# A second head's scores moved by 384 columns in a three-bank PSUM tile, and computed with one matmul fewer

## The chip, the cores and the metric

One core of one Trainium2 chip runs the whole program. The metric is the device time of one execution in microseconds (us). PE is the matrix engine (TensorE), PEld its weight loads, DVE the vector engine, ACT the scalar engine, POOL the GpSimd engine, and SP the engine that issues most DMAs. Matmul results land in PSUM, which here is used in banks of 512 fp32 columns; DVE and ACT read it from there.

## What is computed

Attention on 4 batches, 8 heads, 576 positions and head dimension 64, and behind it two dense stages on the 2304 rows that come out:

```python
q_rot, k_rot = rotate(q), rotate(k)
scores = (1 / sqrt(D)) * q_rot @ k_rot.T            # 576 x 576 for each head
attn = exp(scores - max); attn = attn / (sum + 1e-9)
x = attn @ v                                         # then (B*S) x (H*D) = 2304 x 512
h = maximum(maximum(x @ w1, x @ w2), x @ w3)         # 2304 x 768
x = h @ w_out                                        # 2304 x 512
h = x @ w_in; g = h * sigmoid(h)                     # 2304 x 2048
out = g @ w_out2                                     # 2304 x 512
```

## The kernel before

**Attention.** Heads go in pairs (`hp`, four for a batch): head 0 of a pair lies on partitions 0 to 63 of a tile `T`, head 1 on partitions 64 to 127. The 576 queries of a pair are cut into five tiles, `t` = 0 to 4; the first four have 128 queries for both heads, the fifth (`t` = 4) holds the last 64 queries of both heads and is treated as one head. That makes 16 pairs x 5 = 80 score tiles, 64 of them with two heads. The 576 keys are 512 "main" keys (columns 512 to 1023 of `T`) and 64 left over, which lie for both heads, block-diagonal, in a small tile `K`.

`tile_scores` (L349) computes a two-headed tile into the PSUM tile `s`, 128 partitions x 1536 columns, three banks, of which there is one buffer (`ps_s`, L93). Before, head 0 takes columns 0 to 575 and head 1 columns 576 to 1151. One matmul (L361) with `K` on all 128 partitions gives the 64 leftover columns of both heads, which are neighbours (512 to 639). L364 gives the main keys with 64 partitions for each head: 512 columns for head 0, and for head 1 384 columns (640 to 1023, the end of bank 1) and 128 columns (1024 to 1151, in bank 2). All of it is fp32, and the trace records every fp32 matmul of this kind twice, as two passes, each with a weight load of its own; so L361 has 64 x 2 and L364 has 64 x 3 x 2 records. `t` = 4 tiles use L354 and L355 instead.

`tile_max` (L370) takes the maximum of both heads with one DVE instruction (L374), then one ACT instruction per head computes the exponentials out of PSUM (L381) into the SBUF tile `e` (columns by `HK`, 576 a head). `tile_norm` scales `e` (L393), `tile_turn` transposes it on PE (L408, L413, L422) and evacuates (`pt`, L426, L428), `av` multiplies by V (L437, L441). `qk_turn` (L319) transposes q and k (L328, L334) for the next pair.

**Dense stages.** `moe1` (L510) is fed between the attention steps, by a counter of matmul columns (L947); it is the work that PE does while a score tile waits for its maximum and its exponentials. Its results leave PSUM by L526 and L528 on ACT and DVE. The second dense stage (L778 to L809) begins after the attention and after the last of `moe1`, at about 650 us of the trace.

**What sets the order.** The program is written in one sequence; a scheduler then gives each engine its own row of instructions, by a model of how long each takes. So a change in one matmul can move instructions of other steps past each other on every engine. Within one engine the row is fixed.

Of the kernel before, what the change touches and what calls it, by code (L numbers as in the profile page):

```python
# [11 lines left out]
AF = mybir.ActivationFunctionType  # L12
ALU = mybir.AluOpType
AX = mybir.AxisListType
# [8 lines left out]
def fused_kernel(  # L23
# [22 lines left out]
    nc = tc.nc  # L46
# [297 lines left out]

    s_t, e_t, sum_t, pt_t, exps = {}, {}, {}, {}, []
    HK = (slice(0, 576), slice(576, 1152))
    evacs = [0]

    def tile_scores(key):  # L349
        b, hp, t = key  # L350
        T, K, Q = T_t[b, hp]
        s = ps_s.tile([P, 1536], F32, tag="s", name="s")
        if t == 4:
            nc.tensor.matmul(s[:, 0:512], Q, T[:, 512:1024], start=True, stop=True)  # L354
            nc.tensor.matmul(s[:, 512:576], Q, T[:, 1024:1088], start=True, stop=True)  # L355
            s_t[key] = s
            return
        n = P
        qs = T[:, t * P:t * P + n]
        kt = T[:, 512:1024]  # L360
        nc.tensor.matmul(s[0:n, 512:640], qs, K, start=True, stop=True)  # L361
        for g, o, a, m in ((0, 0, 0, 512), (1, 640, 0, 384), (1, 1024, 384, 128)):
            r = slice(64 * g, 64 * g + 64)
            nc.tensor.matmul(s[0:n, o:o + m], qs[r], kt[r, a:a + m], start=True, stop=True)  # L364
        s_t[key] = s

    def heads(key):
        return 1 if key[2] == 4 else 2

    def tile_max(key):  # L370
        s = s_t.pop(key)
        m = heads(key)
        nb = small.tile([P, 2], F32, tag="nb", name="nb")
        x = nc.vector.tensor_reduce(  # L374
            out=nb[:, 0:m], in_=s[:, 0:576 * m].rearrange("p (h k) -> p h k", h=m), op=ALU.max, axis=AX.X, negate=True
        )
        last["max"] = x.ins
        e = e_p.tile([P, 1152], F32, tag="e", name="e")
        sm = small.tile([P, 2], F32, tag="sm", name="sm")
        for g in range(m):  # L380
            x = nc.scalar.activation(  # L381
                out=e[:, HK[g]], in_=s[:, HK[g]], func=AF.Exp, bias=nb[:, g:g + 1], accum_out=sm[:, g:g + 1]
            )
        exps.append(x.ins)
        e_t[key], sum_t[key] = e, sm

    def tile_norm(key):
# [4 lines left out]
        for g in range(m):  # L392
            nc.scalar.activation(out=e[:, HK[g]], in_=e[:, HK[g]], func=AF.Copy, scale=r[:, g:g + 1])  # L393

# [85 lines left out]
    def attention():  # L480

        for j in range(len(tiles) + 4):
            if j < len(tiles):
                tile_scores(tiles[j])
                tile_max(tiles[j])
            if 1 <= j <= len(tiles):
                tile_norm(tiles[j - 1])
            if 2 <= j <= len(tiles) + 1:
                tile_turn(tiles[j - 2])
            for f, a in events.pop(j, ()):  # L490
                f(*a)
            yield
# [206 lines left out]
    o = 0  # L699
    while o < NT:  # L700
        n = min(512, NT - o)
# [262 lines left out]
    n = 0  # L964
# [63 lines left out]
```

## Time and profile before

| | us |
|---|---|
| median of 3 runs | 1078.11 |
| lowest and highest of them | 1073.08, 1078.49 |
| the profiled execution, its own time | 1072.23 |
| its span (first to last instruction) | 1070.5 |
| PE busy in the span | 984.0 (92%) |
| DVE, ACT, POOL busy | 595.0, 592.0, 370.2 |
| mean granted TensorE clock | 0.971 |

Busy times of PE are unions of overlapping records: matmuls are pipelined, and one record begins before the one ahead of it has ended. What a matmul costs PE is therefore read from the start of one group of instructions to the start of the next, not from the mean duration of a record. The granted clock is 1 at 2.4 GHz and 0.5 at 1.2 GHz.

### The profile page before, as it was taken

What the parts mean: (1) busy time and instruction counts of PE and PEld (TensorE: products, weight loads), DVE (VectorE), ACT (ScalarE), POOL (GpSimd) and SP (SyncE); (2) the same over time, 40 slices, a digit from 0 to 9 for tenths busy, and PEclk for the clock granted to TensorE, in tenths of its full rate; (3) what the DMA queues carried; (4) which work ended last, traced back from release to release, by engine and by line L of the source; (5) the groups of instructions that cost most, each with busy time, mean ns of one, the idle gap of its engine ahead of it and who ended that gap; (6) DMA issues with size and microseconds to landing.
All of it is one profiled execution on the core that took longest, in us unless ns stands there. A gap on an engine that the chain in (4) does not pass through costs nothing.

```text
span 1070.5 us, 19191 instructions
## 1 busy us (share of the span) xinstructions
PE 984.0 (92%) x7554; PEld 761.6 (71%) x7554; DVE 595.0 (56%) x1078; ACT 592.0 (55%) x1298; POOL 370.2 (35%) x396
## 2 busy tenths in 40 slices
PE   2378897999998999989999999999999999999997
PEld 1245574676776677667767567778888888888887
DVE  5858667544476666476456559654532533533432
ACT  3668775646665767756666756464433433433432
POOL 1596125730115741032111211144343433433432
PEclk9678998999999999999999999998999999999999
DMA  7633022310225433223323326110100200100000
GB/s 193 204 111 111 30 90 57 82 24 1 73 85 146 122 95 90 72 73 86 122 60 89 115 68 248 49 64 1 60 10 12 60 16 6 40 21 1 21 21 20
DMA packets 81129, 76.28 MB, mean 71 GB/s; under 512 B 44944, under 2 KB 61840, under 8 KB 80528
## 3 DMA queue, kind: packets, MB, share of 16 engines
q1 hardware_dynamic: 77328, 64.77, 20.7%
q10 hardware_dynamic: 3712, 10.29, 2.9%
q8 instruction: 59, 0.97, 0.4%
q14 instruction: 30, 0.25, 0.1%
HBM read 57.21 MB, written 17.83 MB: 70 GB/s over the span
## 4 chain that ended last, share of the span: by engine, by line
PE 71%; DVE 5%; DMA 3%; POOL 1%; issue 1%; SPq 1%; ACT 1%; DVEq 0%; POOLq 0%; ACTq 0%
PE m L510 18%; PE mb L778 8%; PE m L778 8%; PE xp L441 5%; PE a L809 4%; PE c L809 4%; PE s L364 4%; PE b L809 4%; PE tr L422 4%; PE mg L510 3%; PE d L809 2%; PE xp L437 1%; PE s L361 1%; PE tr L328 1%; PE s L354 1%
## 5 line engine op out<-in xcount | busy, mean ns | idle before, releaser
L785 POOL TENSOR_TENSOR gs<-gs 128x256 f32<-128x256 f32 x144 | 131.4, 913 | 222.0 <-ACT gs L779 216.5
L510 PE MATMUL m<-x,w 128*128 128x256 f16 (+1 forms) x1380 | 197.8, 289 | 6.0 <-DVE t L528 3.2
L510 PEld LDWEIGHTS <-w 128*128 128x128 f16 x1632 | 158.6, 99 | 53.1 <-issue 13.0
L791 DVE SCALAR_TENSOR_TENSOR g<-gs,sg,g 128x768 f16<-128x768 f32 x72 | 97.9, 1362 | 173.4 <-ACT g L790 173.0
L778 PEld LDWEIGHTS <-wi 128*128 128x128 f16 x1656 | 162.0, 98 | 18.7
L809 PEld LDWEIGHTS <-g 128*128 128x128 f16 x1485 | 146.1, 99 | 21.5 <-DVE g L791 3.3
L207 POOL TENSOR_SCALAR z<-z 128x256 uint16<-128x256 uint16 x64 | 54.2, 847 | 256.6 <-DVE z L206 242.1
L374 DVE TENSOR_REDUCE nb<-s 128x2 f32<-128x1152 f32 (+1 forms) x80 | 98.7, 1234 | 63.1 <-PE s L364 48.4
L381 ACT ACTIVATE e<-s,nb 128x576 f32<-128x576 f32 x144 | 105.3, 737 | 46.3 <-DVE nb L374 42.0
L790 ACT ACTIVATE g<-gs,sg 128x768 f16<-128x768 f32 x72 | 74.9, 1041 | 72.2 <-POOL gs L785 71.1
L393 ACT ACTIVATE e<-e,rec 128x576 f32<-128x576 f32 x144 | 104.3, 768 | 17.9 <-DVE rec L391 17.7
L422 PE MATMUL tr<-ident,e 128*128 128x128 f32 x576 | 98.0, 287 | 12.1 <-ACT pt L426 3.1
L778 PE MATMUL mb<-yt,wi 128*128 128x256 f16 x828 | 95.0, 273 | 0.0
L778 PE MATMUL m<-yt,wi 128*128 128x256 f16 x828 | 94.8, 273 | 0.0
L422 PEld LDWEIGHTS tr<-ident,e 128*128 128x128 f32 x576 | 68.6, 145 | 32.8 <-ACT pt L426 5.8
L426 ACT ACTIVATE pt<-tr 128x384 f32<-128x384 f32 x128 | 61.1, 488 | 50.2 <-PE tr L422 49.8
L441 PE MATMUL xp<-pt,vd 128*64 128x256 f32 (+1 forms) x512 | 85.3, 427 | 0.0
L364 PE MATMUL s<-T 64*128 64x512 f32 (+2 forms) x384 | 82.1, 510 | 0.0
L510 PE MATMUL m<-h,wo 128*128 128x256 f16 (+1 forms) x448 | 64.9, 286 | 2.3 <-POOL wo L156 1.2
L364 PEld LDWEIGHTS s<-T 64*128 64x128 f32 x384 | 45.9, 196 | 27.3 <-issue 5.6
L779 ACT ACTIVATE gs<-mb,ch 128x512 f32<-128x512 f32 x36 | 24.7, 686 | 71.9 <-PE mb L778 71.9
L441 PEld LDWEIGHTS xp<-pt,vd 128*64 128x64 f32 x512 | 37.1, 140 | 35.0 <-issue 17.7
(199 smaller groups left out, 1500.0 us busy)
## 6 DMA issues: line engine op xcount, KB each, us to landing
z<-in_moe_w_in_dram SPq DMA_DIRECT2D x32, 256.0 KB, 3.2
z<-in_moe_w_out_dram SPq DMA_DIRECT2D x32, 256.0 KB, 3.2
w<-in_moe_w_dram ACTq DMA_DIRECT2D x6, 768.0 KB, 7.5
wo<-in_moe_w_dram ACTq DMA_DIRECT2D x6, 768.0 KB, 5.5
qk<-in_q_dram SPq DMA_DIRECT2D x32, 128.0 KB, 3.1
qk<-in_k_dram SPq DMA_DIRECT2D x32, 128.0 KB, 3.0
vd<-in_v_dram SPq DMA_DIRECT2D x16, 256.0 KB, 3.0
zwi<-z SPq DMA_DIRECT2D x32, 128.0 KB, 3.1
```

Source lines behind the costliest of these rows:

```text
L364: nc.tensor.matmul(s[0:n, o:o + m], qs[r], kt[r, a:a + m], start=True, stop=True)
L374: x = nc.vector.tensor_reduce(out=nb[:, 0:m], in_=s[:, 0:576 * m].rearrange("p (h k) -> p h k", h=m), op=ALU.max, axis=AX.X, negate=True)
L381: x = nc.scalar.activation(out=e[:, HK[g]], in_=s[:, HK[g]], func=AF.Exp, bias=nb[:, g:g + 1], accum_out=sm[:, g:g + 1])
L393: nc.scalar.activation(out=e[:, HK[g]], in_=e[:, HK[g]], func=AF.Copy, scale=r[:, g:g + 1])
L422: nc.tensor.transpose(tr[:, i * n:(i + 1) * n], e[0:n, c * P:(c + 1) * P], ident[0:n, 0:n])
L441: nc.tensor.matmul(xp[r, 0:n], v4[:, g, c, :], pt[:, c + 5 * g, :], start=False, stop=(c == 3))
L510: nc.tensor.matmul(ps[:, 0:n], l, r, start=(i == 0), stop=(i == len(passes) - 1))
L778: nc.tensor.matmul(ps[:, e * 256:e * 256 + 256], l, r, start=(i == 0), stop=(i == len(passes) - 1))
L785: nc.gpsimd.tensor_tensor(out=g[o], in0=g[x], in1=g[y], op=op)
L790: nc.scalar.activation(out=h, in_=x, func=AF.Copy, scale=sg)
L791: nc.vector.scalar_tensor_tensor(out=l, in0=x, scalar=sg, in1=h, op0=ALU.mult, op1=ALU.subtract)
L809: x = nc.tensor.matmul(ps, l, r, start=first, stop=last_, skip_group_check=True)
```

## The change

Head 1's scores stand in columns 960 to 1535: its 64 leftover columns at 960 to 1023, at the end of bank 1, and its 512 main columns at 1024 to 1535, which is bank 2. Its main keys take one matmul of 512 columns in place of 384 + 128. The matmul of the leftover keys now writes two runs of 64 columns, 448 apart (512 to 575 and 960 to 1023). The maximum reads two runs of 576 columns that begin 960 apart, and the exponentials of head 1 read from 960; `e` in SBUF keeps its layout. Tiles with `t` = 4 are as before.

```diff
+    SK = (slice(0, 576), slice(960, 1536))
+
+    def both(s, o, step, n):
+
+        return bass.AP(tensor=s.tensor, offset=s.offset + o, ap=[list(s.ap[0]), [step, 2], [1, n]])
...
-        nc.tensor.matmul(s[0:n, 512:640], qs, K, start=True, stop=True)
-        for g, o, a, m in ((0, 0, 0, 512), (1, 640, 0, 384), (1, 1024, 384, 128)):
+        nc.tensor.matmul(both(s, 512, 448, 64), qs, K, start=True, stop=True)
+        for g, o in ((0, 0), (1, 1024)):
             r = slice(64 * g, 64 * g + 64)
-            nc.tensor.matmul(s[0:n, o:o + m], qs[r], kt[r, a:a + m], start=True, stop=True)
+            nc.tensor.matmul(s[:, o:o + 512], qs[r], kt[r], start=True, stop=True)
...
-            out=nb[:, 0:m], in_=s[:, 0:576 * m].rearrange("p (h k) -> p h k", h=m), op=ALU.max, axis=AX.X, negate=True
+            out=nb[:, 0:m], in_=both(s, 0, 960, 576) if m > 1 else s[:, 0:576], op=ALU.max, axis=AX.X, negate=True
...
-                out=e[:, HK[g]], in_=s[:, HK[g]], func=AF.Exp, bias=nb[:, g:g + 1], accum_out=sm[:, g:g + 1]
+                out=e[:, HK[g]], in_=s[:, SK[g]], func=AF.Exp, bias=nb[:, g:g + 1], accum_out=sm[:, g:g + 1]
```

Line numbers behind the new lines are 5 higher: L366 is the matmul of the leftover keys, L369 that of the main keys, L379 the maximum, L427 the transposes of `e`. In a row, `s_1643` is a score tile, `tr_...` a transpose's PSUM tile, `m_...` a group of `moe1` or of a small reduction (L113); numbers of tiles differ between the two programs.

PE, tile `t` = 0 of batch 1, head pair 0 (its scores begin at 177.65 us of the trace). Before:

```order
L441 MATMUL xp_1539<-pt_1230,vd_0_122 64x320 x8
L361 MATMUL s_1643<-kd_0_116,T_1360 128x128
L364 MATMUL s_1643<-T_1360 128x512
L364 MATMUL s_1643<-T_1360 128x384
L422 MATMUL tr_1534<-ident_78,e_1337 128x128 x3
L328 MATMUL tr_1552<-ident_78,qk_840 128x128 x4
L113 MATMUL m_1585<-ident_78,wm_2_1583 1x128
L364 MATMUL s_1643<-T_1360 128x128
```

and the same place now:

```order
L446 MATMUL xp_1523<-pt_1216,vd_0_122 64x320 x8
L366 MATMUL s_1627<-kd_0_116,T_1345 128x2x64
L369 MATMUL s_1627<-T_1345 128x512 x2
L427 MATMUL tr_1518<-ident_78,e_1322 128x128 x3
L328 MATMUL tr_1536<-ident_78,qk_829 128x128 x4
L113 MATMUL m_1569<-ident_78,wm_2_1567 1x128
```

Before, the scheduler had put eight other matmuls between the second and the third of the L364 matmuls; now the two stand together. Of the 64 two-headed tiles, 7 had their L364 matmuls apart in this way before (5 with the last one apart, 2 with the first one apart), and 3 have their two L369 matmuls apart now.

PE, tile `t` = 3 of batch 3, head pair 0 (at 564.20 us of the trace of before). Before:

```order
L422 MATMUL tr_6061<-ident_78,e_5861 128x128 x3
L361 MATMUL s_6040<-kd_0_116,T_4883 128x128
L364 MATMUL s_6040<-T_4883 128x512
L364 MATMUL s_6040<-T_4883 128x384
L364 MATMUL s_6040<-T_4883 128x128
L422 MATMUL tr_6066<-ident_78,e_5861 128x128 x3
```

and now:

```order
L515 MATMUL m_6117<-x_3729,w_0_131 128x320
L366 MATMUL s_5983<-kd_0_116,T_4836 128x2x64
L369 MATMUL s_5983<-T_4836 128x512
L427 MATMUL tr_5898<-ident_78,e_5712 128x128 x3
L369 MATMUL s_5983<-T_4836 128x512
L515 LDWEIGHTS w_0_131
```

Here the three stood together, and now three transposes stand between the two heads.

DVE, tile `t` = 0 of batch 1, head pair 3 (its scores begin at 227.33 us of the trace), with the maximum `nb`, the evacuations `pt` and `t`, and the low half `h`. Before:

```order
L535 TENSOR_TENSOR h_7_2044<-t_2042,h_7_2044 128x320
L428 COPY pt_2000<-tr_2088 128x3x128
L528 SCALAR_TENSOR_TENSOR t_2106<-m_2093,t_2060 128x320
L374 TENSOR_REDUCE nb_2131<-s_2126 128x2
L528 SCALAR_TENSOR_TENSOR t_2121<-m_2108,t_2106 128x320
```

and now:

```order
L540 TENSOR_TENSOR h_7_2023<-t_2021,h_7_2023 128x320
L379 TENSOR_REDUCE nb_2108<-s_2104 128x2
L433 COPY pt_1979<-tr_2066 128x3x128
L533 SCALAR_TENSOR_TENSOR t_2084<-m_2071,t_2039 128x320
L396 RECIPROCAL rec_2187<-rec_2187 128x2
```

The maximum stood behind an evacuation of a transpose and one of `moe1`, and stands ahead of both now. PE's row keeps its order at the beginning (to 57 us of the trace of before), from about 150 to 190 us, and behind the attention (from about 600 us); between these stretches, groups of `moe1` stand up to 24 matmuls earlier or later against the score tiles. The waits that each score tile has are the same ones: on the exponentials of the tile before, at its first matmul.

## Rows read from the trace of the kernel before

**Rows 1.** The page, parts 1 and 2: PE's busy time, granted clock.

```profile
PE 984.0 (92%) x7554; PEld 761.6 (71%) x7554; DVE 595.0 (56%) x1078; ACT 592.0 (55%) x1298; POOL 370.2 (35%) x396
...
PE   2378897999998999989999999999999999999997
...
PEclk9678998999999999999999999998999999999999
```

**Rows 2.** Busy by stage; columns: length, engines, PEclk, DMA share, GB/s.

```profile
60.00:130.00 70.00, 55.70 (x312) 34.41 (x312) 47.88 (x83) 54.86 (x123) 39.99 (x34) 0.90 0.30 93
...
190.00:320.00 130.00, 128.50 (x923) 91.58 (x923) 65.04 (x130) 80.53 (x205) 34.52 (x37) 1.00 0.19 53
320.00:490.00 170.00, 160.13 (x1136) 114.63 (x1135) 110.44 (x248) 107.59 (x295) 70.08 (x73) 0.99 0.35 100
490.00:620.00 130.00, 125.43 (x863) 87.55 (x860) 76.07 (x179) 89.25 (x249) 22.54 (x27) 0.99 0.33 96
```

**Rows 3.** Groups by form: the matmuls and the maximum that the change touches.

```profile
L374 DVE TENSOR_REDUCE nb<-s 128x2 f32<-128x1152 f32 x64 | 86.7, 1355 | 48.9 <-PE s L364 48.4
L364 PE MATMUL s<-T 64*128 64x512 f32 x128 | 76.6, 680 | 0.0
...
L364 PE MATMUL s<-T 64*128 64x384 f32 x128 | 61.8, 565 | 0.0
...
L364 PE MATMUL s<-T 64*128 64x128 f32 x128 | 26.2, 286 | 0.0
...
L374 DVE TENSOR_REDUCE nb<-s 128x1 f32<-128x576 f32 x16 | 12.0, 752 | 14.2 <-PE s L355 14.1
```

**Rows 4.** Timeline of PE, a score tile with its matmuls together.

```profile
405.43 0.38 PE L361 MATMUL s<-kd,T 128*128 128x128 f32 x2
405.74 1.14 PE L364 MATMUL s<-T 64*128 64x512 f32 x6
406.81 1.40 PE L510 MATMUL m<-x,w 128*128 128x320 f16 x9
```

**Rows 5.** Timeline of PE, a tile whose third L364 matmul stands apart.

```profile
178.07 1.12 PE L364 MATMUL s<-T 64*128 64x512 f32 x4
179.12 0.55 PE L422 MATMUL tr<-ident,e 128*128 128x128 f32 x3
179.50 0.60 PE L328 MATMUL tr<-ident,qk 128*128 128x128 f32 x4
179.94 0.27 PE L113 MATMUL m<-ident,wm 128*1 128x128 f32 x1
180.14 0.49 PE L364 MATMUL s<-T 64*128 64x128 f32 x2
180.56 0.66 PE L328 MATMUL tr<-ident,qk 128*128 128x128 f32 x4
```

**Rows 6.** Timeline of PE, a tile whose two heads stand apart.

```profile
334.47 1.12 PE L364 MATMUL s<-T 64*128 64x512 f32 x2
335.53 0.65 PE L328 MATMUL tr<-ident,qk 128*128 128x128 f32 x4
336.11 1.13 PE L364 MATMUL s<-T 64*128 64x384 f32 x4
337.17 0.38 PE L116 MATMUL m<-amax,ones 1*128 1x1 f32 x2
```

**Rows 7.** Timeline of PE, the second pass of one L361 alone.

```profile
405.54 0.28 PE L361 MATMUL s<-kd,T 128*128 128x128 f32 x1
```

**Rows 8.** Source L361 from 130 to 640 us: what PE waits for.

```profile
  ACT e L381: 2.4, 7
```

**Rows 9.** Timeline of PE: from one tile's exponentials to the next tile's scores.

```profile
574.97 1.26 PE L510 MATMUL m<-x,w 128*128 128x320 f16 x8
576.07 0.49 PE L422 MATMUL tr<-ident,e 128*128 128x128 f32 x3
576.40 2.06 PE L510 MATMUL m<-x,w 128*128 128x320 f16 x14
578.30 0.38 PE L361 MATMUL s<-kd,T 128*128 128x128 f32 x2
```

**Rows 10.** Timeline of ACT: the exponentials that those scores wait for.

```profile
574.23 0.74 ACT L381 ACTIVATE e<-s,nb 128x576 f32<-128x576 f32 x1 [1.75 <-DVE nb L374]
```

## The prediction

> **What bounds the kernel now.** I read the page first: PE is busy for 984.0 us of a span of 1070.5, and the next engine, DVE, for 595.0 [rows 1]. Busy time of PE does not say that PE is the limit in every stage, so I then read the table by stage. In the four stretches in which attention and the first dense stage run mixed and the order of PE's instructions changes, PE is idle for 14.3, 1.5, 9.9 and 4.6 us, 30.3 us in all (length minus PE busy) [rows 2]; the clock is below 1 mostly in the first. So from 130 us on PE is the bound, and a microsecond of PE time there is a microsecond of the program. Third, I looked for the wait that the change could shorten in another way: the scores of a tile need the one `s` buffer, so their first matmul waits for the exponentials of the tile before. From 130 to 640 us PE (weight loads and matmuls) was held up by these for 2.4 us in all, 7 times [rows 8]. That chain (maximum, exponentials, next scores) is hidden behind `moe1` there, and making it shorter is worth nearly nothing. What counts is the PE time of the score matmuls themselves, and where other instructions land.
>
> **The third L364 matmul.** The form table invites a sum: a pass of 384 columns has a mean of 565 ns, of 128 columns 286, of 512 columns 680 [rows 3]; 565 + 286 - 680 = 171 ns, for 64 tiles x 2 passes 21.9 us. That sum is wrong, because records overlap, and because head 0 (partitions 0 to 63) and head 1 (64 to 127) run at the same time. The timeline shows it: all six passes of a tile take from 405.74 to 406.81, 1.07 us, until the next group starts [rows 4]. Head 0 alone, two passes, takes 1.06 us (334.47 to 335.53), and head 1 alone, four passes, also 1.06 (336.11 to 337.17) [rows 6]. A tile without its 128-column matmul takes 1.05 (178.07 to 179.12) [rows 5]. So the two heads run side by side, and the third matmul costs 0.01 to 0.02 us where it stands beside the others. 512 columns for both heads cannot be faster than one head alone, 1.05 to 1.06, so a tile gains 0.01 to 0.02 us. 57 of the 64 tiles have their matmuls together: 0.6 to 1.1 us, I take 0.8. At the lower clock at the beginning both heads stretch alike, so nothing more comes from there.
>
> The Trainium skill, "TensorEngine Tiling (Array Packing)", section "Instruction Overhead", gives about 60 cycles of overhead for every matmul; at 2.4 GHz that is an estimate of 25 ns, and for the 128 passes that go 3.2 us in place of my 0.8. The 0.01 to 0.02 us per tile of rows 4 and 5, which hold two such passes, speak against that sum here.
>
> **Score matmuls that stood apart.** Where the scheduler puts other matmuls between the parts, the overlap is lost. Third matmul apart: the tile's first part takes 1.05 (against 1.07), the two 128-column passes 0.42 alone (180.14 to 180.56), and they start 0.20 after the matmul ahead, where a transpose follows a transpose after 0.11 (0.44 for four, from 179.50), so 0.09 more [rows 5]. Together 1.05 + 0.42 + 0.09 - 1.07 = 0.49 us. Heads apart: 1.06 + 1.06 + 0.09 - 1.07 = 1.14 us [rows 6]. Before, 5 tiles were of the first kind and 2 of the second: 5 x 0.49 + 2 x 1.14 = 4.7 us. Now 3 are of the second kind: 3 x 1.14 = 3.4 us. That saves 1.3 us.
>
> **The products with V** (L441) overlap in pairs in the same way, and the new order cuts them elsewhere. I counted the places at which a pair is broken in the two orders: 17 in both. That is no gain and no loss.
>
> **The strided output of the leftover keys.** L361's matmul keeps 128 columns and two passes, but writes two runs of 64. No matmul in this trace writes in runs, so the cost is bounded. Below: nothing, and no gain, since the same columns go through. Above: as if each pass were done twice, at the distance of its passes, 0.11 us (405.43 to 405.54 [rows 4, 7]): 128 x 0.11 = 14.1 us. I take 0, since a pass is fed by its 128 columns, and these stay.
>
> **Maximum and exponentials** read as many elements as before. Should the longer step cost DVE as much as two instructions would, that is 2 x 752 - 1355 = 149 ns for each of 64 [rows 3], 9.5 us of DVE, which is busy for 110 of 170 us where it is busiest of the last three stretches [rows 2]; it would lengthen the hidden chain by 0.15 us a tile. I take 0. The cover of that chain: after tile `t` = 4 at 574 us, the exponentials end at 574.23 + 0.74 = 574.97, and the next scores start at 578.30, so 3.3 us of slack, filled with 22 `moe1` matmuls at 0.136 us (1.90 / 14 from 576.40) [rows 9, 10]. In the new order this same place has 15 of these fewer, 2.0 us, and 1.3 us of slack are left. The largest other shifts there are also 12 to 18 matmuls; where they eat the slack, the price is under 2 us each, and the work that is moved is done elsewhere.
>
> **The sum.** 0.8 + 1.3 = 2.1 us off PE, nothing added. Against the profiled execution: 1072.23 - 2.1 = 1070.1. That execution is 5.9 us below the median of the runs, and the four times known (1072.23, 1073.08, 1078.11, 1078.49) lie in two pairs. 2.1 below the median is 1076.0; 2.1 below the middle of all four (1075.6) is 1073.5. Between these I forecast **1075**.
>
> **What the new order does to the waits** is the larger unknown. In the stretches with a new order PE loses 30.3 us to waits and, by the granted clock (0.90 in 70 us, 0.99 in 170 and in 130 us), 7.0 + 1.7 + 1.3 = 10.0 us to the lower clock [rows 2]. These 40 us are dealt again: the places at which PE's row meets a late evacuation shift, and with a PE pause the clock can go. Nothing in the trace gives a sign. Most of these losses should come back in kind; that a quarter, 10 us, goes or comes is the bound that I use.
>
> **Rivals.**
> 1. *The waits fall better.* For it: the two tiles in which a `moe1` group stood before the last score matmul are whole now, and in one of them the maximum is ahead of two evacuations on DVE. Against it: the chain was hidden already [rows 8]. 1075 - 10 = 1065.
> 2. *Records do not overlap as I read them,* and the 171 ns are real: 1075 + 2.1 - 21.9 = 1055. Rows 4 to 6 speak against it.
> 3. *The strided write slows L366*, slower than before: place, the 128 passes of L366; price, up to 14.1 us, so 1075 + 14.1 = 1089. It decides from (5.4 + 2.1) / 128 = 0.06 us more for a pass, which is half a doubling. Nothing in the trace speaks for it, but nothing shows such a write either.
> 4. *The waits fall worse*, with a lower clock after a new pause: 1075 + 10 = 1085.
>
> **How the numbers follow.** A measurement of this kernel can tell about 0.5%, 5.4 us, from no change: below 1072.7 is faster, above 1083.5 slower. Forecast 0.61, with a range of its own of 1069 to 1081; rival 1 0.21; rival 2 0.02; rival 3 0.07; rival 4 0.09. Faster: rival 1 nearly whole (0.18), rival 2, and 0.15 of the forecast, whose range reaches below 1072.7: 0.35. Slower: 0.05 of rival 3, 0.06 of rival 4, 0.01 of the forecast: 0.12. Same: 0.53. For the range I leave out rival 2, half of rivals 3 and 4 each and the lower half of rival 1, 0.2 in all: 1065 to 1084.
>
> **What would show it.** In the profile after: a tile's two L369 matmuls (four passes) take 1.05 to 1.06 us until the next start; L366's two passes still start 0.11 us apart, and L369 follows 0.31 after the first; three tiles with heads apart at about 1.06 each; 128 matmuls and 128 weight loads fewer; DVE's maximum at 1355 ns. PE busy should fall by 2 us plus or minus what overlaps. The forecast is wrong if PE's idle time between 60 and 620 us, or its clock, changes by more than some 5 us, or if L366 takes longer.

## The result, and the profile after

The changed kernel takes 1067.24 us (median of 6 runs, 1063.98 to 1069.74), against 1078.3 us of the kernel before beside it (6 runs): a ratio of 0.9911, interval 0.9888 to 0.9934, or 9.6 us less. In the prediction's terms that is faster (below 1072.7), to which it gave a chance of 0.35; its first choice was no change that can be told, with 0.53. The forecast was 1075; the time lies inside its range and near its rival 1 (1065, "the waits fall better").

The page of after (its own time is 1066.3 us, its mean granted clock 0.972) answers to [rows 1]:

```profile
span 1064.6 us, 18923 instructions
PE 979.2 (92%) x7426; PEld 737.5 (69%) x7426; DVE 594.4 (56%) x1078; ACT 591.2 (56%) x1298; POOL 371.3 (35%) x396
```

128 matmuls and 128 weight loads are gone (7554 to 7426), as they should be, and PE is busy for 4.8 us less. The table by stage of after (length, busy us and instructions of PE, PEld, DVE, ACT and POOL, granted clock, DMA share, GB/s) answers to [rows 2]:

```profile
60.00:130.00 70.00, 54.73 (x310) 31.75 (x310) 49.16 (x87) 55.07 (x126) 41.03 (x36) 0.95 0.29 93
...
190.00:320.00 130.00, 128.61 (x901) 87.40 (x900) 66.00 (x129) 79.96 (x203) 32.88 (x36) 1.00 0.19 55
320.00:490.00 170.00, 161.06 (x1094) 110.09 (x1093) 109.28 (x246) 108.60 (x298) 70.09 (x74) 0.96 0.35 98
490.00:620.00 130.00, 126.92 (x851) 83.22 (x849) 78.08 (x181) 90.57 (x251) 22.60 (x27) 1.00 0.33 96
```

PE's idle time in these stretches is 15.3, 1.4, 8.9 and 3.1 us, 28.7 against 30.3, and the clock takes 3.5 + 6.8 = 10.3 us against 10.0. Read so, nothing has moved. But a stretch of fixed times holds other work after than before, since the work slides; stretches must be cut by the work. The table below does that, from the start of the first score matmul of one tile to that of another.

**What the change touches directly.** The forms of after, which answer to [rows 3] (line, engine, form, count, busy us, mean ns, idle before):

```profile
L369 PE MATMUL s<-T 64*128 64x512 f32 x256 | 81.3, 687 | 0.0
L366 PE MATMUL s<-kd,T 128*128 128x128 f32 x128 | 28.0, 302 | 9.7 <-ACT e L386 9.6
```
```profile
L379 DVE TENSOR_REDUCE nb<-s 128x2 f32<-128x1152 f32 x64 | 86.7, 1355 | 39.0 <-PE s L369 38.6
```

The strided matmul of the leftover keys has a mean of 302 ns and 28.0 us in all; L361 in the kernel before has the same two numbers (302, 28.0). The maximum over two runs of 576 columns, 960 apart, has 1355 ns, as it had over neighbours. PE's timeline of after (start us, us, instruction; a row joins passes), a tile with its two heads together, and one with them apart:

```profile
402.48 0.39 PE L366 MATMUL s<-kd,T 128*128 128x128 f32 x2
402.80 1.13 PE L369 MATMUL s<-T 64*128 64x512 f32 x4
403.86 0.72 PE L515 MATMUL m<-x,w 128*128 128x320 f16 x4
```
```profile
337.15 1.12 PE L369 MATMUL s<-T 64*128 64x512 f32 x2
338.20 0.66 PE L328 MATMUL tr<-ident,qk 128*128 128x128 f32 x4
338.79 1.12 PE L369 MATMUL s<-T 64*128 64x512 f32 x2
339.84 0.38 PE L116 MATMUL m<-amax,ones 1*128 1x1 f32 x2
```

Both heads together take 402.80 to 403.86, 1.06 us; before, with the third matmul, 1.07 [rows 4]. Apart, each takes 1.05, against 1.06 in [rows 6]. So four passes of 512 columns, two heads of 64 partitions, cost what two passes cost.

### The profile page after: what moved, and what is told of

Its sections match the earlier page's. It is cut to its first block, busy times and chain, and to the rows that moved or that the text cites. A ratio compares the mean times of both kernels' runs of the same rounds, so it can differ in the third digit from the quotient of the medians.

```text
span 1064.6 us, 18923 instructions
## 1 busy us (share of the span) xinstructions
PE 979.2 (92%) x7426; PEld 737.5 (69%) x7426; DVE 594.4 (56%) x1078; ACT 591.2 (56%) x1298; POOL 371.3 (35%) x396
## 4 chain that ended last, share of the span: by engine, by line
PE 72%; DVE 4%; DMA 2%; ACT 2%; POOL 1%; issue 1%; SPq 1%; POOLq 0%; DVEq 0%; ACTq 0%
PE m L515 19%; PE mb L783 8%; PE m L783 8%; PE xp L446 5%; PE s L369 4%; PE tr L427 4%; PE a L814 4%; PE c L814 4%; PE b L814 4%; PE mg L515 3%; PE d L814 2%; PE xp L442 1%; PE s L366 1%; PE s L359 1%; PE tr L328 1%
## 5 line engine op out<-in xcount | busy, mean ns | idle before, releaser
L515 PEld LDWEIGHTS <-w 128*128 128x128 f16 x1632 | 158.9, 99 | 65.5 <-issue 27.2
L379 DVE TENSOR_REDUCE nb<-s 128x2 f32<-128x1152 f32 (+1 forms) x80 | 98.8, 1234 | 58.6 <-PE s L369 38.6
L427 PE MATMUL tr<-ident,e 128*128 128x128 f32 x576 | 96.9, 286 | 12.0 <-DVE pt L433 4.3
L427 PEld LDWEIGHTS tr<-ident,e 128*128 128x128 f32 x576 | 68.9, 145 | 48.9 <-issue 15.8
L369 PE MATMUL s<-T 64*128 64x512 f32 x256 | 81.3, 687 | 0.0
L515 PEld LDWEIGHTS <-wo 128*128 128x128 f16 x512 | 49.1, 98 | 21.8 <-issue 5.3
```

Of the source, the lines that this page charges most:

```text
L369: nc.tensor.matmul(s[:, o:o + 512], qs[r], kt[r], start=True, stop=True)
L379: x = nc.vector.tensor_reduce(out=nb[:, 0:m], in_=both(s, 0, 960, 576) if m > 1 else s[:, 0:576], op=ALU.max, axis=AX.X, negate=True)
L427: nc.tensor.transpose(tr[:, i * n:(i + 1) * n], e[0:n, c * P:(c + 1) * P], ident[0:n, 0:n])
L515: nc.tensor.matmul(ps[:, 0:n], l, r, start=(i == 0), stop=(i == len(passes) - 1))
```

## The experiments

**The changed kernel again**, beside further runs of the kernel before.

> The changed kernel once more, as the measure for the three runs beside it. Ratio to the kernel before 0.991 (0.989 to 0.993), as first measured.

Measured: 1067.92 us (6 runs), ratio 0.9914 (0.9885 to 0.9943). The gain of 9 us stands, and so it is several times what the score matmuls can give.

**Matmuls and order apart, first attempt.** The order of an engine can be held by a dependency from each instruction to the one behind it on the same engine, with no wait added:

```diff
+def _freeze(tc):
...
+    for n in order:
...
+        if e in last:
+            tc.add_manual_dep(i, last[e].name, info, reason="order")
+        last[e] = i
```

> The changed kernel's instructions, but every engine's row in the order of the kernel before (without the third score matmul). If the gain comes from the order (waits and clock dealt again), only the matmuls' own part is left: 62 tiles with both heads together at 0.007 us each and the five third matmuls no longer apart at 0.49 us, 2.9 us, ratio 0.997 (0.995 to 0.999). If the matmuls themselves are worth the 10 us (fewer passes and weight loads than the timeline lets one see), the ratio is 0.991 as for the changed kernel.

> The kernel before, three score matmuls a tile and the old columns, but every engine's row in the order of the changed kernel, the third matmul right behind the second. If the gain is the order's, it is here too: 0.4 us more than the changed kernel, ratio 0.991 to 0.993. If the matmuls themselves are worth it, the ratio is 0.998 to 1.000.

> The kernel before in its own order, with one difference: in the seven tiles whose score matmuls stood apart the later ones stand right behind the first. By the prices of the timeline, 5 x 0.49 + 2 x 1.14 = 4.7 us less, ratio 0.9957 (0.994 to 0.998). If waits swallow what PE gains there, 0.999 to 1.001.

Measured: 1603.24 us (ratio 1.4878, 1.4836 to 1.492), 1602.91 (1.488, 1.4839 to 1.4919) and 1604.11 (1.4897, 1.4851 to 1.4943). All three expectations failed for a reason outside the theories: the rows held here were those in which the program is written, not those that the scheduler had made of it. The page of the first, and PE's largest wait in it (engine, line, releaser: us, times, longest):

```profile
PE 1131.4 (71%) x7426; PEld 808.4 (50%) x7426; DVE 589.0 (37%) x1078; ACT 604.1 (38%) x1298; POOL 352.6 (22%) x396
```
```profile
PE tr L427 <- ACT pt L431: 288.3, 64, 9.5
```

At each of the 64 two-headed tiles a transpose waits some 4.5 us (288.3 / 64) for the evacuation of an earlier one. These runs say nothing about the change's order, but one thing about scale: between this order and the scheduler's lie some 530 us in this kernel. And where the tiles' matmuls stand together in one order, three matmuls or two make no difference that shows (1602.91 and 1603.24).

**Matmuls and order apart, second attempt**, with the scheduler's rows of the two kernels held. In the traces of these runs the rows of DVE and ACT, and PE's apart from the score matmuls, are instruction for instruction those of the kernel that the order comes from. First: the new matmuls in the old order, and the old matmuls in the new order (the third matmul behind the second).

> The changed kernel's instructions, with every engine's row in the scheduled order of the kernel before (the run of this name before this one had the order as written, not as scheduled). Theory 'order': most of the 9 us comes from waits and clock in the new order; then only the matmuls' own part is left, 62 tiles at 0.007 us and five third matmuls no longer apart at 0.49 us, 2.9 us, ratio 0.997 (0.995 to 0.999). Theory 'matmuls': the matmuls themselves are worth it, ratio 0.991.

> The kernel before (three score matmuls a tile, old columns), with every engine's row in the scheduled order of the changed kernel, the third matmul right behind the second. Theory 'order': the gain is here too, 0.4 us short of the changed kernel, ratio 0.991 to 0.993. Theory 'matmuls': 0.998 to 1.000.

Then each order with its split tiles put together. One of the seven places in the old order, and one of the three in the new:

```diff
 L364 MATMUL s_1643<-T_1360 128x512
 L364 MATMUL s_1643<-T_1360 128x384
+L364 MATMUL s_1643<-T_1360 128x128
 L422 MATMUL tr_1534<-ident_78,e_1337 128x128 x3
 L328 MATMUL tr_1552<-ident_78,qk_840 128x128 x4
 L113 MATMUL m_1585<-ident_78,wm_2_1583 1x128
-L364 MATMUL s_1643<-T_1360 128x128
...
 L369 MATMUL s_5983<-T_4836 128x512
+L369 MATMUL s_5983<-T_4836 128x512
 L427 MATMUL tr_5898<-ident_78,e_5712 128x128 x3
-L369 MATMUL s_5983<-T_4836 128x512
```

> The kernel before in its own scheduled order, with one difference: in the seven tiles whose score matmuls stood apart the later ones stand right behind the first. By the prices of the timeline 5 x 0.49 + 2 x 1.14 = 4.7 us less, ratio 0.9957 (0.994 to 0.998). If waits swallow what PE gains, 0.999 to 1.001. If these places are the whole of the gain (each also ends a wait further on), 0.991.

> The changed kernel in its own scheduled order, with the three tiles whose two heads stand apart made whole. By the timeline 3 x 1.14 = 3.4 us less than the changed kernel: ratio to the kernel before 0.988 (0.986 to 0.991), profile span about 1062 to 1064 us. If waits swallow it, 0.991 as the changed kernel.

Measured, as ratios to the kernel before:

| | old order | new order |
|---|---|---|
| old matmuls | 1 | 0.9893 (0.9862 to 0.9924), 1063.16 us |
| new matmuls | 0.9958 (0.9932 to 0.9984), 1071.67 us | 0.9911 and 0.9914 (above) |
| no tile split | 0.9943 (0.9915 to 0.9971), 1069.85 us, old matmuls | 0.9896 (0.9867 to 0.9924), 1063.77 us, new matmuls |

The old matmuls in the new order have the whole gain. The new matmuls in the old order have 0.4%, which is what they should give there: 0.8 us for the third matmul and 5 x 0.49 for the five tiles that it split, 3.2 us or 0.3%. Putting all seven tiles of the old order together was priced at 4.7 us (0.9957) and gave 0.9943. Putting the three tiles of the new order together was priced at 3.4 us (0.988) and gave 0.9896; its interval holds that as well as no gain over the changed kernel. So the times agree with the prices, within intervals of 0.3% to either side, and the rest of the gain is the order. The kernel before, held in its own rows, was not run; but held kernels compared with each other, less the prices, still put the new order 5 to 10 us ahead of the old one, so the gain does not come from the holding.

**Where it is.** The trace of each kernel, cut at the starts of the first score matmul of tiles 20, 40 and 79 (80 tiles, counted from 0 in order of time). In brackets, PE's idle time and the time lost to the half clock (half the length of each stretch at it); all from one profile each:

| | tile 20 to 40, us | tile 40 to 79, us |
|---|---|---|
| before | 156.5 (6.6, 0.0) | 289.1 (11.6, 3.4) |
| new matmuls, old order | 155.0 (5.4, 1.7) | 292.8 (13.3, 6.8) |
| old order, none split | 155.1 (5.7, 1.7) | 292.5 (13.1, 8.5) |
| after | 160.2 (8.6, 3.4) | 283.6 (7.2, 3.4) |
| after again | 159.8 (8.6, 3.4) | 283.7 (9.0, 1.7) |
| old matmuls, new order | 157.6 (7.3, 1.7) | 281.4 (8.1, 0.0) |
| new order, none split | 157.6 (7.3, 1.7) | 280.6 (7.7, 3.4) |

From tile 40 to 79 the old order takes 289 to 293 us and the new one 281 to 284; idle time and clock together are 15.0 to 21.6 us in the old and 8.1 to 11.1 in the new. From tile 20 to 40 the new order is the slower one, by 1 to 5 us. Before tile 20 the new order is 1 to 3 us shorter (175.4 to 176.9 against 177.6 to 178.2); after tile 79 there is no steady difference. Idle time and clock taken off, tile 20 to 79 takes 424.0 us in before and 2.1 to 5.9 us less in the six others, each within 1.1 us of its direct price (that of its matmuls and splits). So the prices are PE's work, and the order's part lies in waits and clock.

One profile is not a kernel's median. That of before took 1072.23 us, 3 to 6 below the medians beside the runs; that of the old order with none split took 1075.64, 5.8 above its median. Between the profiles of before and after, idle time and clock from tile 20 to 79 come to 21.6 and 22.6 us: what after gains behind tile 40 it loses ahead of it, and this pair does not show the order's gain. The two kernels that cross matmuls and order (new matmuls in the old order, old ones in the new) do: their profiles (1071.55 and 1063.87) lie within 1 us of their medians, and idle time and clock there are 27.2 us in the old order and 17.1 in the new one.

The largest single place behind tile 40 is at 477 us. In before, PE (idle time and its releaser in brackets at the end) and DVE there:

```profile
476.06 0.27 PE L414 MATMUL tr<-ident,e 128*64 128x128 f32 x1
477.19 0.27 PE L113 MATMUL m<-ident,vm 128*1 128x128 f32 x1 [0.86 <-DVE t L528]
477.30 0.49 PE L422 MATMUL tr<-ident,e 128*128 128x128 f32 x3
480.23 2.08 PE L510 MATMUL m<-x,w 128*128 128x256 f16 x9 [2.44 <-DVE t L528]
```
```profile
475.81 1.00 DVE L206 TENSOR_SCALAR z<-z 128x256 f32<-128x256 f32 x1 [0.96 <-DMA z<-in_moe_w_out_dram]
476.73 0.41 DVE L528 SCALAR_TENSOR_TENSOR t<-m,t 128x256 f32<-128x256 f32 x1
477.06 0.75 DVE L220 TENSOR_SCALAR z<-z 128x256 int32<-128x256 int32 x1
477.73 1.08 DVE L206 TENSOR_SCALAR z<-z 128x256 f32<-128x256 f32 x1
478.85 0.81 DVE L220 TENSOR_SCALAR z<-z 128x256 int32<-128x256 int32 x1
479.58 0.27 DVE L206 TENSOR_SCALAR z<-z 128x256 f32<-128x256 f32 x1
479.77 0.41 DVE L528 SCALAR_TENSOR_TENSOR t<-m,t 128x256 f32<-128x256 f32 x1
```

PE needs two evacuations of `moe1` (L528). On DVE the first stands behind an L206, the narrowing of the dense weights, which waits for its transfer, and the second behind four more instructions of that narrowing. The same place after:

```profile
476.90 0.27 PE L113 MATMUL m<-ident,vm 128*1 128x128 f32 x1 [0.23 <-DVE t L533]
...
480.63 0.38 PE L116 MATMUL m<-amax,ones 1*128 1x1 f32 x2 [1.48 <-DVE amax L115]
```
```profile
476.42 0.88 DVE L533 SCALAR_TENSOR_TENSOR t<-m,t 128x256 f32<-128x256 f32 x2
479.80 0.58 DVE L206 TENSOR_SCALAR z<-z 128x256 f32<-128x256 f32 x1 [2.50 <-DMA z<-in_moe_w_out_dram]
480.31 0.27 DVE L115 TENSOR_REDUCE amax<-m 1x1 f32<-1x128 f32 x1
```

Both evacuations (now L533) stand ahead of the L206. DVE waits longer for the transfer, 2.50 us, and PE only 0.23 + 1.48 in place of 0.86 + 2.44. In the old order with no tile split the pause is 1.48 + 2.44:

```profile
476.10 0.27 PE L113 MATMUL m<-ident,vm 128*1 128x128 f32 x1 [1.48 <-DVE t L528]
476.21 0.49 PE L422 MATMUL tr<-ident,e 128*128 128x128 f32 x3
479.13 2.72 PE L510 MATMUL m<-x,w 128*128 128x256 f16 x12 [2.44 <-DVE t L528]
```

There the clock is near half over the next 11 us, in before and after only for a part of them (the granted clock stands behind POOL's busy time). That kernel, before, and after:

```profile
478.00:489.00 11.00, 9.87 (x38) 5.20 (x38) 5.51 (x16) 3.10 (x10) 5.16 (x6) 0.53 0.28 72
```
```profile
478.00:489.00 11.00, 8.77 (x52) 5.51 (x52) 7.31 (x20) 3.26 (x10) 6.44 (x7) 0.84 0.26 72
```
```profile
478.00:489.00 11.00, 8.98 (x49) 5.00 (x48) 8.51 (x20) 4.57 (x13) 9.76 (x11) 0.84 0.44 132
```

With the clock (1 less 0.53 or 0.84, times 11 us) this place costs 3.3 + 1.8 = 5.1 us in before, 3.9 + 5.2 = 9.1 in the old order with none split, and 1.7 + 1.8 = 3.5 after, 1.6 and 5.6 us less.

The second place is at 537 us. Before, and after, PE and DVE:

```profile
537.02 0.43 PE L510 MATMUL m<-x,w1f 128*128 128x320 f16 x2 [1.99 <-DVE t L528]
...
533.94 2.29 DVE L146 TENSOR_REDUCE ym<-yr 128x1 f32<-128x2048 f32 x1 [2.21 <-DMA yr<-yscr]
...
536.48 0.48 DVE L528 SCALAR_TENSOR_TENSOR t<-m,t 128x320 f32<-128x320 f32 x1
```
```profile
536.67 0.43 PE L515 MATMUL m<-x,w1f 128*128 128x320 f16 x2 [1.18 <-DVE t L533]
...
533.61 2.29 DVE L146 TENSOR_REDUCE ym<-yr 128x1 f32<-128x2048 f32 x1 [0.98 <-DMA yr<-yscr]
```

Here the evacuation stands behind an instruction that waits for a transfer (L146, a maximum over rows read back for the second dense stage) in both orders, but that wait is shorter after. In before the clock is at half for 3.4 us from 537.8 on, after it stays full: 2.0 + 1.7 = 3.7 us against 1.2. The two places hold 4.1 of the 4.4 us by which idle time and clock differ between before and after from tile 40 to 79. In the pair that crosses matmuls and order they hold 10.5 of 12.0 (from 470 to 489 and from 530 to 545 us, 9.5 and 5.0 us in the old order, 3.3 and 0.7 in the new one). The others are small: a wait of 1.6 us on POOL (357 us in before) is gone in the new order, one of 1.6 on DVE (349 us after) is new. All this is read from the traces; no run changed either place alone.

**One move in the new order.** Where the new order loses, at 322 us, the same pattern stands the other way round. After, PE and DVE:

```profile
327.00 2.72 PE L515 MATMUL m<-x,w 128*128 128x256 f16 x12 [4.84 <-DVE t L533]
```
```profile
321.74 0.85 DVE L540 TENSOR_TENSOR h<-t,h 128x256 f16<-128x256 f32 x1
324.75 1.74 DVE L206 TENSOR_SCALAR z<-z 128x256 f32<-128x256 f32 x2 [2.16 <-DMA z<-in_moe_w_in_dram]
326.53 0.43 DVE L533 SCALAR_TENSOR_TENSOR t<-m,t 128x256 f32<-128x256 f32 x1
```

The edit, on DVE, in the new order with no tile split:

```diff
 L540 TENSOR_TENSOR h_7_3158<-t_3156,h_7_3158 128x256
+L533 SCALAR_TENSOR_TENSOR t_3189<-m_3176,t_3174 128x256
 L206 TENSOR_SCALAR z_3128<-z_0_3031 128x256
 L206 TENSOR_SCALAR z_3138<-z_1_3131 128x256
-L533 SCALAR_TENSOR_TENSOR t_3189<-m_3176,t_3174 128x256
```

> The new order with the three split tiles put together (as in the run of that, 0.9896 of before, span of its profile 1059.5 us), and one DVE instruction moved: the evacuation of a moe1 group (L533) that stood behind two instructions that wait for a transfer of the second dense stage's weights (L206) stands ahead of them. In three profiles of the new order PE was idle there, at about 322 us, for 3.5 to 4.8 us. Theory (the order makes the time by such single places): this gap shrinks to under 1 us, nothing else moves, 2.7 to 4 us less, a ratio of about 0.986 to 0.987, some 1060 to 1061 us. Rival (the wait only moves on to the next place that is late): a gap of the same length within 20 us behind it, ratio 0.989 to 0.990.

Measured: 1060.76 us (6 runs), ratio 0.9865 (0.9841 to 0.9889). PE and DVE there now:

```profile
322.82 1.47 PE L515 MATMUL m<-x,w 128*128 128x256 f16 x12 [1.09 <-DVE t L533]
...
326.96 0.52 PE L427 MATMUL tr<-ident,e 128*128 128x128 f32 x3 [2.44 <-DVE pt L416]
```
```profile
322.35 0.42 DVE L533 SCALAR_TENSOR_TENSOR t<-m,t 128x256 f32<-128x256 f32 x1
323.27 2.01 DVE L206 TENSOR_SCALAR z<-z 128x256 f32<-128x256 f32 x2 [0.50 <-DMA z<-in_moe_w_in_dram]
325.20 1.28 DVE L220 TENSOR_SCALAR z<-z 128x256 int32<-128x256 int32 x2
326.40 0.41 DVE L416 COPY pt<-tr 128x256 f32<-128x256 f32 x1
```

In the trace the rival is right: the gap at 322 shrinks to 1.09, and the evacuation L416 behind the narrowing takes up the rest, 2.44 us four microseconds on. 1.09 + 2.44 is the 3.47 of the run that it was made from. The time says 3 us less, but the two intervals (0.9841 to 0.9889, 0.9867 to 0.9924) overlap; what differs in the profiles is the clock, which lost 1.7 us from tile 20 to 40 and 3.4 from 40 to 79 in that run, and nothing here. Whether the move helps stays open, and with it what one such place is worth. As it stands this is the fastest kernel measured: 0.9865 of before, against 0.9911 for the changed kernel.

**Old order at the beginning, new one behind.** Up to tile 36 every engine's old row and new row hold the same instructions, so the rows can be changed there. Edit: the rows held are the old ones before tile 36 and the new ones from it, no tile split, with the move above.

> The new matmuls, none split, and the same moved evacuation as in the run beside it; but the rows of all engines are the old ones until score tile 36 (about 300 us) and the new ones from there. Theory (the gain over the old order lies between tile 40 and tile 79): tile 40 to tile 79 takes 280 to 284 us, as in every profile of the new order, against 289 to 293 in the old one; tile 20 to tile 40 takes 152 to 155 us (the old order's 155 or so, less what the moved evacuation gives if its wait was the new order's). In all the ratio is 0.983 to 0.987, 0 to 3 us below the run beside it. Rival (the gain isn't local: what the new order does before 300 us, loads that start earlier or groups of moe1 done ahead, makes the stretch behind it faster): tile 40 to tile 79 takes 288 us or more, ratio 0.992 to 0.996.

Measured: 1061.75 us, ratio 0.9878 (0.9851 to 0.9904). Tile 40 to 79 takes 278.2 us, so the rival falls: the stretch is short whatever order stands ahead of 300 us, and the gain is in the rows of that stretch itself. The second number missed, and the ratio lies just above the 0.983 to 0.987 expected. Tile 20 to 40 took 159.1 us where 152 to 155 were expected; 5.1 us of it are lost to the half clock, which the estimate had left as in the other runs.

**The order dealt anew by other edits.** Is the new order good because of what the change does, or would any edit do? Two edits of the kernel before that leave the same matmuls and let the scheduler make the order again. First, head 1 ahead of head 0:

```diff
-        for g, o, a, m in ((0, 0, 0, 512), (1, 640, 0, 384), (1, 1024, 384, 128)):
+        for g, o, a, m in ((1, 640, 0, 384), (1, 1024, 384, 128), (0, 0, 0, 512)):
```

> The kernel before, with its three L364 matmuls written in another sequence: head 1 first, then head 0. The same instructions with the same work; the scheduler deals the order anew. By the timeline's prices the splits are worth about +4 us against before (9 tiles split in place of 7). Theory (any small rewriting deals the waits anew, with either sign, and the change's order drew a good one): the time differs from 1.0 plus 0.004 by some 5 us in either direction, and tile 40 to tile 79 has its own length, anywhere from 280 to 293 us. Rival (the gain belongs to what the change does, three matmuls becoming two as the scheduler's model counts them): no gain here, ratio 1.002 to 1.007, with tile 40 to tile 79 at 289 us or more, as before.

Second, the leftover keys last:

```diff
-        nc.tensor.matmul(s[0:n, 512:640], qs, K, start=True, stop=True)
         for g, o, a, m in ((0, 0, 0, 512), (1, 640, 0, 384), (1, 1024, 384, 128)):
             r = slice(64 * g, 64 * g + 64)
             nc.tensor.matmul(s[0:n, o:o + m], qs[r], kt[r, a:a + m], start=True, stop=True)
+        nc.tensor.matmul(s[0:n, 512:640], qs, K, start=True, stop=True)
```

> The kernel before, with the matmul of the leftover keys (L361) written behind the three L364 matmuls in place of ahead of them. The same instructions with the same work; the scheduler deals the order anew. By the timeline's prices the splits are worth about nothing against before. Theory (any small rewriting deals the waits anew): a second draw, 1.0 plus or minus 5 us or more, with tile 40 to tile 79 anywhere from 280 to 293 us; the first pass of head 0 can start without waiting for anything else than L361 did, so nothing else changes. Rival (the gain belongs to the change's own matmuls): 0.998 to 1.002, tile 40 to tile 79 at 289 us or more.

Measured: 1079.76 us, ratio 1.0039 (1.0018 to 1.0061), with 288.1 us from tile 40 to 79; and 1065.64 us, ratio 0.9908 (0.9884 to 0.9932), with 283.5 us. The first has the ratio of the rival there: the splits, priced at about 4 us, are the whole difference. Yet this new order is not like the old one in every stretch. Tile 40 to 79 is 0.9 us under the rival's 289, with only 11.4 us of idle time and clock in it, and tile 20 to 40 takes 165.0 us, against 156.5 before. The second has the full gain of the change with none of its matmuls, which the rival did not allow. Its splits are not worth nothing, as was expected: in its trace four tiles have the third matmul apart and none has its heads apart, 4 x 0.49 = 2.0 us against 4.7, so 2.7 us of its gain are direct and some 7 are the order's. So the order's gain does not belong to the wider bank or to the matmul saved; another edit finds it too, and a third does not. In both traces the clock stays full from 340 to 620 us. Three new orders, two of them with the gain, are no distribution: how often an edit would win by it stays open.

## Why the prediction was right or wrong, point by point

- **Bound by PE, chain hidden:** right. From 130 to 640 us of the trace of after the first score matmuls and their weight loads wait 1.6 us for exponentials, 5 times, against 2.4 us and 7 times [rows 8].
- **The third matmul:** right. 1.07 became 1.06 us a tile; the records' sum of 21.9 us, rival 2, was no cost. The Trainium skill, "TensorEngine Tiling (Array Packing)", section "Instruction Overhead", with its about 60 cycles for a matmul would make it some 0.05 us a tile by estimate; the two timelines differ by 0.01.
- **Score matmuls that stood apart:** right in kind and size: 4.7 us predicted for the seven tiles of the old order, 0.57% or 6.1 us measured (interval 0.29 to 0.85%).
- **The products with V:** right. PE's time in them, from the start of each run of them to the next start, is 81.4 us in both traces.
- **The strided output, maximum and exponentials:** right, at nothing: 302 ns and 302, 1355 and 1355. Rival 3 falls.
- **What the new order does to the waits** is the step that failed, by its size. It was named as the larger unknown, bounded at 10 us, and set to nothing in the forecast, on the ground that "Nothing in the trace gives a sign" and that "Most of these losses should come back in kind". The forecast's own sum has 2.1 of the 9.6 us; that the time lies in the range is owed to rival 1, half of which the range took in. The prediction had little reason for that sign (0.21 for better waits, 0.09 for worse), so this much of it is luck. Taking the direct prices off each measured difference (at 1076 us) leaves:

| | measured, us | direct, by the prediction's prices | left for the order |
|---|---|---|---|
| after, and again | -9.6, -9.3 | -2.1 | -7.5, -7.2 |
| old matmuls, new order | -11.5 | -1.3 | -10.2 |
| new order, none split | -11.2 | -5.5 | -5.7 |
| new matmuls, old order | -4.5 | -3.2 | -1.3 |
| old order, none split | -6.1 | -4.7 | -1.4 |
| leftover keys last | -9.9 | -2.7 (from its trace) | -7.2 |
| heads swapped | +4.2 | +4 | 0 |

With some 3 us of uncertainty each, the change's order is worth 6 to 10 us and the old order, held, none. That is what rival 1 said, and its price was 10. The reason that it gave is not borne out: at 227 us, where the maximum now stands ahead of two evacuations, no matmul waits for another engine in either trace (225 to 234 us). The places that the traces show are evacuations of `moe1` behind DVE instructions that wait for a transfer, at 477 and 537 us; that they are the cause is read there and not tested one by one.
- **The sign that was there.** The prediction looked at the new order where the scores and the maximum are. Among the longest pauses of PE behind 190 us in the trace of before are those of 0.86 and 2.44 us at 477 us, both on L528, with the instruction that held the releaser up in DVE's row beside them; the new order shows both evacuations ahead of it, and at 322 us one behind it. That look would have given a sign for single places, of both directions. It would not have given the sum: the gain in the two profiles is 1.6 us of idle time at 477 us and 0.8 at 537, where the rows show nothing of it, and the loss at 322 us is 2.6 (4.84 after, against 1.40 and 0.83 before).
- **What would have shown it wrong:** "if PE's idle time between 60 and 620 us, or its clock, changes by more than some 5 us". By fixed times neither did, though the order was the cause. The test was badly cut: stretches must follow the work, not fixed times.

## What to carry to other kernels

Two matmuls on different halves of the partitions run side by side (here 1.06 us for both heads, 1.05 for one), so a matmul saved on one side alone is worth next to nothing: read its cost from start to start, not from the records. Where a scheduler deals the order anew, treat the order as a change of its own with its own size (here 0.6 to 0.9% against 0.2% for the matmuls), and separate the two by holding one order for both; else the edit gets a credit that another edit would have had as well. To see the order's part ahead of time, take the longest pauses one by one and look at what stands in front of their releaser in the new rows, above all instructions that wait for a transfer. That gives candidates and not a sum: here the one move that was tried only handed the wait on to the next evacuation.

## What the runs showed of the hardware

A pause of PE does not fix what the clock does behind it. In the second dense stage, where both kernels do the same work, PE pauses for 3.07 us in before and 3.06 after; the 8 us behind it are here in before and then after:

```profile
722.00:730.00 8.00, 6.88 (x38) 4.99 (x39) 6.53 (x5) 4.20 (x5) 5.03 (x4) 0.57 0.00 0
```
```profile
719.00:727.00 8.00, 6.89 (x63) 6.18 (x64) 6.52 (x5) 4.21 (x5) 5.03 (x4) 1.00 0.01 2
```

The clock is 0.57 in one and 1.00 in the other, with PE busy for the same time, and 38 matmuls are done in place of 63. That is 3 us of the difference between these two profiles that belongs to neither order; the same pause is followed by stretches at half clock of 3.4 us in the unsplit new order and of 6.8 in before. So single profiles of this kernel differ by such stretches, and only the timed medians carry the last 3 us.

That a matmul may write two runs of columns, 448 apart, at no cost (302 ns a pass either way) was assumed and is now measured.
